# A recurrent transformer step rewritten in a fixed order by halves of heads, with part of its QKV moved into one dense pass and 42 of 64 weight chunks resident

## The chip, the cores and the metric

The kernel runs on one core of a Trainium2 chip. The metric is the device time of one execution in microseconds (us), on the slowest core, which here is the only one. Before the change the median of three runs was 2933.01 us (2913.09 to 2933.23). "The change" and "after" mean the kernel with the change; "before" the one without.

## The reference, cut to what matters

The program computes two independent outputs and puts them side by side. Part A is a long convolution by FFT; the change does not touch it, and it ends at about 279 us. Part B, the rest of the time, is this recurrence (cut):

```python
S, Dm, H, Dh, M, seg = 2048, 1024, 32, 128, 8, 32
mem = mem0                                   # 8 memory tokens
for s in range(64):                          # 64 segments of 32 tokens
    h = concat([mem, x[s*32:(s+1)*32]])      # 40 tokens x 1024
    q, k, v = h @ Wq, h @ Wk, h @ Wv         # 32 heads of 128
    p = softmax(mask(q @ k.T * Dh**-0.5))    # 40 x 40 for each head
    o = (p @ v) @ Wo                         # 40 x 1024
    mem = o[:8]                              # goes into the next segment
    outs.append(o[8:])                       # 32 tokens of output
```

Each segment needs all four weights (32 MB in bf16), and the segments follow each other through `mem`. Both kernels cut the weights into 64 chunks of 128 x 2048 (512 KB), keep some in SBUF for good ("resident") and stream the others from HBM in every segment through a ring of buffers. Both kernels feed the PE array 32 tokens at a time, so each segment's last 8 tokens are extra work and are treated apart; they don't depend on `mem` before attention.

## The kernel before

38 chunks are resident, 26 are streamed in each segment, through a ring of six. The tile scheduler orders the instructions. The last 8 tokens of the four segments of a block are taken together, as a second set of 32 rows, in the block's last segment. The softmax covers all heads in one go. The outputs are stored from the POOL (GpSimd) queue.

```python
NRES, RING = 38, 6
ring = tc.tile_pool(name="b_ring", bufs=RING)

def wchunk(m, i):
    if i in res_slot[m]:
        return res_tiles[m][:, res_slot[m][i], :]
    t = ring.tile([128, CW], BF, tag="wring", name="wchunk")
    nc.sync.dma_start(dst_view(t[:], m), dram_chunk(m, i))              # L508
    return t[:]

def qkv_pass(pairs, m, extra=None):          # pairs: this segment, and at a
    ...                                      # block's end its last 8 tokens x 4
    for kc in range(8):
        for hf in range(CPK):
            w = wchunk(m, CPK * kc + hf)
            for pi, (hT_ap, dst_sb) in enumerate(pairs):
                ...
                nc.tensor.matmul(accs[pi][g][32 * c:32 * c + 32, :], lhsT=hT_ap[:, kc, :],
                                 rhs=w[:, jl * 512:(jl + 1) * 512], ...) # L536
...
for s in range(n_seg):
    ...
    qkv_pass(qpairs, 0); qkv_pass(kpairs, 1)
    ...
    softmax(SA, masks[("A", j)], PA_pad)     # 128 x 512, all heads
    softmax(SC, masks[("C", j)], PC_pad)
    ...
    wo_pass(opairs)                          # matmuls yacc, L561
    ...
    for dq in range(4):
        nc.gpsimd.dma_start(outb[SEG * s:SEG * s + 24, dq * 256:(dq + 1) * 256],
                            Y_sb[32 * dq + 8:32 * dq + 32, :])          # L721
```

## Time and profile before

| | before |
|---|---|
| median | 2933.01 us |
| first segment's result Y copied out of PSUM | at 372.4 us |
| one segment after it (Y to Y, mean of 63) | 40.24 us |
| last segment of a block of four / the others | 45.0 / 37.3 to 39.5 us |
| bytes moved, 560 to 2860 us | 345 GB/s |

These lines are from the page of before: its span, the busy time of each engine (PE is TensorE's matmuls, PEld its weight loads, DVE VectorE, ACT ScalarE, POOL GpSimd; L508 is line 508 of the kernel), the DMA engines' busy share in 40 equal slices of the span (tenths), and the chain of waits that ended last, by engine and by line.

```profile
span 2926.3 us, 80950 instructions
...
PE 2062.4 (70%) x36046; PEld 1129.8 (39%) x36052; DVE 924.1 (32%) x1936; ACT 631.6 (22%) x1191; POOL 377.6 (13%) x714
...
DMA  7886999999999999999899998999999999999996
...
PE 40%; DMA 33%; DVE 16%; ACT 5%; issue 2%; POOL 1%; SPq 0%; ACTq 0%; DVEq 0%; POOLq 0%
DMA wchunk<-in_B_Wq_dram 17%; PE yacc L561 11%; DMA wchunk<-in_B_Wk_dram 9%; PE OTp L698 4%; PE OTp L701 3%; PE qk_tp L548 3%; DVE Ppads L592 2%; DVE ssum L590 2%; DVE mx L586 2%; ACT KA_sb L541 2%; DMA wchunk<-in_B_Wv_dram 2%; DVE SA L582 1%; ACT QA_sb L541 1%; DVE SA L587 1%; DVE SC L582 1%
```

From the fifth slice on, the DMA engines stand at 8 or 9 tenths to the last but one, while PE is busy for 70%. The chain has PE on 40% of its length and DMA on 33%. Two of its three costliest entries are loads of streamed weights, 17% and 9% of the span. So the kernel goes back and forth between the stream and PE.

The table of stretches of before shows the whole recurrence, then two short stretches inside one segment. Columns: the stretch in us, its length, busy us and instructions of PE, PEld, DVE, ACT and POOL, the granted clock (PEclk, the share of TensorE's full clock that it was given), the DMA share and GB/s.

```profile
core 0: us, PE busy (x) PEld busy (x) DVE busy (x) ACT busy (x) POOL busy (x), PEclk, DMA share, GB/s
560.00:2860.00 2300.00, 1697.20 (x31501) 953.87 (x31493) 640.27 (x1371) 412.53 (x847) 258.10 (x537) 0.85 0.95 345
1213.00:1217.00 4.00, 4.00 (x92) 3.09 (x85) 0.10 (x1) 0.00 (x0) 0.00 (x0) 0.58 0.61 205
1225.00:1241.00 16.00, 10.55 (x208) 4.60 (x211) 3.47 (x6) 2.34 (x4) 0.00 (x0) 1.00 1.02 408
```

The stream reaches 408 GB/s while PE waits for it (last line), but at 1213 to 1217 us it is down to 205. Just ahead of that PE had waited for DVE's softmax (from 1200.5 to 1208.6 us in the chain of waits) and used no chunks, so the ring was full: from 1200 to 1217 us SyncE's queue waited for PE to free a buffer for 10.4 us in all. The mean of 345 lies between. What SyncE's DMA queue, which issues the loads, waited for says the same (columns: us in total, times, longest):

```profile
SPq L508 <- PE yacc L561: 512.8, 346, 8.6
SPq L508 <- DMA wchunk<-in_B_Wq_dram: 192.2, 272, 2.8
```

The load at L508 waits mostly for matmuls, which must free a buffer of the ring: 512.8 us for those of the output projection (yacc), and 578 us for those of Q, K and V, which the view lists tile by tile. The chain of waits through the same segment, as start, length and what:

```profile
1212.82 4.50 DMA wchunk<-in_B_Wo_dram
1217.32 8.85 DMA wchunk<-in_B_Wq_dram
1226.21 0.42 PE acc_17966 L536 x4
1226.65 7.29 DMA wchunk<-in_B_Wk_dram
```

A piece such as "8.85 DMA wchunk" runs from the issue of a load to PE's use of it. With six loads in the ring one of them takes 7 to 9 us (512 KB at 408 GB/s are 1.28 us): it queues behind the others, and six at 1.28 us are 7.7. Over the whole run the loads land 6.8 to 8.1 us after their issue (medians for the four weights, from before's list of DMA issues).

### The profile page before, as it was taken

Reading aid. Unit: us, or ns where it says so; the run is one execution under the profiler, and the core shown is the slowest. Engines: PE = TensorE matmul, PEld = TensorE weight load, DVE = VectorE, ACT = ScalarE, POOL = GpSimd, SP = SyncE. Lnnn points to the kernel's source line nnn. Section 1 sums busy time; section 2 is a strip of 40 time slices with the busy share of each in tenths; the row PEclk is TensorE's granted clock in tenths of the full one; section 3 lists DMA queues with packets and bytes.
Section 4 is the critical chain, followed back from the end, with each engine's and each line's share of the span. In section 5 each row is a group of like instructions: output and inputs, shape, how many; then the busy total and the mean of one; then the engine's idle time right before and its main releaser. Section 6 shows DMA issues by size and latency. Waiting matters only on the chain.

```text
span 2926.3 us, 80950 instructions
## 1 busy us (share of the span) xinstructions
PE 2062.4 (70%) x36046; PEld 1129.8 (39%) x36052; DVE 924.1 (32%) x1936; ACT 631.6 (22%) x1191; POOL 377.6 (13%) x714
## 2 busy tenths in 40 slices
PE   3665477687776767676867777776868677777775
PEld 1221134343443434343434444343434344443433
DVE  6895122232222222222322222322232222322221
ACT  6771111121111111111111111111112111111211
POOL 4142001001010101010010101010100101010101
PEclk8897678798888889888888888798888788887977
DMA  7886999999999999999899998999999999999996
GB/s 244 305 304 229 375 334 334 341 342 362 347 335 347 331 356 345 352 331 345 330 359 351 339 350 334 348 348 363 321 349 335 348 344 332 359 335 351 348 347 234
DMA packets 356981, 979.09 MB, mean 335 GB/s; under 512 B 42556, under 2 KB 47708, under 8 KB 356631
## 3 DMA queue, kind: packets, MB, share of 16 engines
q1 hardware_dynamic: 329896, 942.33, 88.2%
q0 software_dynamic: 21504, 21.04, 2.3%
q10 hardware_dynamic: 5232, 10.55, 1.1%
q8 instruction: 282, 4.62, 0.6%
q14 instruction: 67, 0.55, 0.1%
HBM read 940.19 MB, written 33.55 MB: 333 GB/s over the span
## 4 chain that ended last, share of the span: by engine, by line
PE 40%; DMA 33%; DVE 16%; ACT 5%; issue 2%; POOL 1%; SPq 0%; ACTq 0%; DVEq 0%; POOLq 0%
DMA wchunk<-in_B_Wq_dram 17%; PE yacc L561 11%; DMA wchunk<-in_B_Wk_dram 9%; PE OTp L698 4%; PE OTp L701 3%; PE qk_tp L548 3%; DVE Ppads L592 2%; DVE ssum L590 2%; DVE mx L586 2%; ACT KA_sb L541 2%; DMA wchunk<-in_B_Wv_dram 2%; DVE SA L582 1%; ACT QA_sb L541 1%; DVE SA L587 1%; DVE SC L582 1%
## 5 line engine op out<-in xcount | busy, mean ns | idle before, releaser
L536 PEld LDWEIGHTS <-hT 128*32 128x32 bf16 x12288 | 390.8, 101 | 853.2 <-issue 614.6
L698 PE MATMUL OTp<-PTs,VA_sb 32*128 32x64 bf16 x2048 | 205.7, 232 | 143.4 <-DVE PTs L687 143.4
L549 DVE COPY QT_sb<-qk_tp 128x1024 bf16<-128x1024 bf16 x80 | 55.3, 692 | 769.7 <-PE qk_tp L548 769.7
L561 PEld LDWEIGHTS <-OT_sb 128*32 128x32 bf16 x8192 | 259.9, 121 | 82.0 <-issue 10.7
L561 PE MATMUL yacc<-Wres_2789,OT_sb 128*32 128x256 bf16 x4608 | 288.4, 338 | 1.4 <-issue 1.4
L561 PE MATMUL yacc<-wchunk,OT_sb 128*32 128x256 bf16 x3584 | 263.2, 354 | 7.1 <-DMA wchunk<-in_B_Wo_dram 5.7
L698 PEld LDWEIGHTS <-VA_sb 32*128 32x128 bf16 x2048 | 181.0, 120 | 194.1 <-issue 154.4
L721 POOL DMA_DIRECT2D out_dram<-Y_sb x256 | 128.2, 508 | 858.2 <-ACT Y_sb L565 568.0
L605 POOL COPY hT<-XT_sb 128x192 bf16<-128x192 bf16 x64 | 22.2, 347 | 1416.7 <-issue 1040.3
L549 DVE COPY KT_sb<-qk_tp 128x1024 bf16<-128x1024 bf16 x80 | 55.2, 689 | 462.3 <-PE qk_tp L548 462.3
L701 PE MATMUL OTp<-PTs,VB_sb 32*128 32x64 bf16 x2048 | 196.7, 232 | 0.5
L701 PEld LDWEIGHTS <-VB_sb 32*128 32x128 bf16 x2048 | 182.8, 122 | 0.0
L536 PEld LDWEIGHTS <-hTB 128*32 128x32 bf16 x3072 | 130.9, 98 | 70.3 <-issue 6.7
L704 ACT CAST OT_sb<-OTp 128x256 bf16<-128x256 f32 x256 | 94.9, 372 | 276.9 <-PE OTp L701 276.6
L612 DVE COPY hT<-mt_tp 128x64 bf16<-128x64 bf16 x64 | 12.3, 191 | 405.4 <-PE mt_tp L611 405.4
L726 POOL DMA_DIRECT2D out_dram<-YB_sb x256 | 126.7, 501 | 65.5 <-DMA out_dram<-Y_sb 29.4
L705 DVE CAST OTB<-OTp 128x64 bf16<-128x64 f32 x256 | 57.6, 225 | 206.0 <-ACT OT_sb L704 205.7
L565 ACT CAST Y_sb<-yacc 128x256 bf16<-128x256 f32 x64 | 23.8, 372 | 366.7 <-PE yacc L561 366.7
L548 PE MATMUL qk_tp<-ident,KA_sb 128*128 128x128 bf16 x512 | 52.6, 228 | 70.6 <-ACT KA_sb L541 70.2
L588 ACT ACTIVATE SA<-SA 128x512 f32<-128x512 f32 x64 | 37.2, 582 | 285.9 <-DVE SA L587 253.6
L548 PE MATMUL qk_tp<-ident,QA_sb 128*128 128x128 bf16 x512 | 62.3, 259 | 50.9 <-ACT QA_sb L541 50.9
L548 PEld LDWEIGHTS <-QA_sb 128*128 128x128 bf16 x512 | 35.6, 112 | 132.1 <-ACT QA_sb L541 120.4
(1731 smaller groups left out, 3917.7 us busy)
## 6 DMA issues: line engine op xcount, KB each, us to landing
wchunk<-in_B_Wv_dram SPq DMA_DIRECT2D x448, 512.0 KB, 6.8
wchunk<-in_B_Wo_dram SPq DMA_DIRECT2D x448, 512.0 KB, 7.5
wchunk<-in_B_Wq_dram SPq DMA_DIRECT2D x384, 512.0 KB, 7.0
wchunk<-in_B_Wk_dram SPq DMA_DIRECT2D x384, 512.0 KB, 8.1
SK_61<-s_sb SPq DMA_DIRECT2D x16, 512.0 KB, 4.7
SU_60<-s_sb SPq DMA_DIRECT2D x16, 512.0 KB, 3.5
Kg<-SK_61 ACTq DMA_DIRECT2D x32, 256.0 KB, 5.1
Ug<-SU_60 SPq DMA_DIRECT2D x32, 256.0 KB, 5.7
```

The lines of the kernel that those rows point to most:

```text
L536: nc.tensor.matmul(accs[pi][g][32 * c:32 * c + 32, :], lhsT=hT_ap[:, kc, :], rhs=w[:, jl * 512:(jl + 1) * 512], start=(kc == 0), stop=(kc ...
L541: nc.scalar.copy(dst_sb[:, g * 512:(g + 1) * 512], accs[pi][g][:])
L548: nc.tensor.transpose(tp[:, idx * 128:(idx + 1) * 128], src_sb[:, idx * 128:(idx + 1) * 128], ident[:])
L549: nc.vector.tensor_copy(dst[:, :, :, col0:col0 + 32], tp[:].rearrange("p (i c r) -> p i c r", i=8, c=4))
L561: nc.tensor.matmul(accs[pi][32 * dq:32 * dq + 32, 0:256], lhsT=OTsrc[:, c, idx, :], rhs=w[:, hh * 1024 + dq * 256:hh * 1024 + (dq + 1) * 256],
L582: nc.vector.scalar_tensor_tensor(out=S3, in0=S3, scalar=scale, in1=mask[:].unsqueeze(1).to_broadcast([128, 8, 64]), op0=ALU.mult, op1=ALU.add)
L586: nc.vector.tensor_reduce(out=mx[:], in_=S3, op=ALU.max, axis=AX.X)
L698: nc.tensor.matmul(OTp[:, idx, :], lhsT=VA_sb[32 * c:32 * c + 32, col:col + 128], rhs=PTA[32 * c:32 * c + 32, idx, :], start=True, stop=False,
L701: nc.tensor.matmul(OTp[:, idx, :], lhsT=VB_sb[32 * c:32 * c + 32, col:col + 128], rhs=PTB[32 * c:32 * c + 32, idx, :], start=False, stop=True,
L704: nc.scalar.copy(OT_sb[:, c, :, :], OTp[:, :, 0:32])
L721: nc.gpsimd.dma_start(outb[SEG * s:SEG * s + 24, dq * 256:(dq + 1) * 256], Y_sb[32 * dq + 8:32 * dq + 32, :])
L726: nc.gpsimd.dma_start(outb[SEG * ss + 24:SEG * ss + 32, dq * 256:(dq + 1) * 256], YB_sb[32 * dq + 8 * jj:32 * dq + 8 * jj + 8, :])
```

## The change

The intent is to take work and bytes out of a segment and pay for it once, ahead of the recurrence:

- K, Q and V of the last 8 tokens of all 64 segments are computed in one dense pass of 768 matmuls of 128 x 128 by 512 columns ahead of the recurrence. The results go to DRAM, and each segment reads its part back (256 KB in seven small reads).
- 42 chunks are resident instead of 38, so 22 are streamed instead of 26. The ring falls from six to four. 24 of the residents ("late") take the memory that the dense pass had used, and are loaded when it has ended.
- The recurrence is in a fixed order instead of the scheduler's, by halves of 16 heads, so that one half's softmax runs beside the other half's projections. The softmax pass is 128 x 320.
- Y is stored in one transfer, from ScalarE's (ACT) queue instead of POOL's.

Part B is rewritten in whole; this is the core of the diff, with cuts marked by "..." and a few comments with line numbers added:

```diff
+NSTREAM = 22
+NEARLY = 18
+RING = 4
...
-    NRES = cfg.get("nres", 38)
-    RING = cfg.get("ring", 6)
...
+        for m in (0, 1):                       # dense pass: K and Q, then V alike
+            for g in range(2):
+                ws = group(m, g)
+                stage = st.tile([128, n_seg, 16, 8], BF, tag="stage", name="stage")
+                for hl in range(16):
+                    ps = ps0.tile([128, 512], F32, tag="ps0", name="kb_ps")
+                    for kc in range(8):
+                        nc.tensor.matmul(ps[:], lhsT=ws[kc][:, hl * 128:(hl + 1) * 128],
+                                         rhs=XBT[:, kc].rearrange("p s t -> p (s t)"), ...)
...
+                nc.sync.dma_start(dst[g], stage[:].rearrange("p s h t -> p s (h t)"))
...
+    def fetch():
+        n = len(loaded)
+        if n < len(uses):
+            t = ring.tile([128, 2048], BF, tag="wring", name="wring")
+            nc.sync.dma_start(dst_view(t[:], uses[n]), dram_chunk(uses[n]))      # L554
+            loaded.append(t)
...
+    def load_x(s):
+        hT = two.tile([128, 8, SEG], BF, tag="hT", name="hT")
+        nc.sync.dma_start(hT[:].rearrange("p k t -> p (k t)"), XTD[:, s]...)     # L575
+        KBs = two.tile([128, 2, 128], BF, tag="KBs", name="KBs")
+        nc.sync.dma_start(KBs[:], KBD[:, :, s, :].rearrange("g p n -> p g n"))
+        QBs = two.tile([128, 288], BF, tag="QBs", name="QBs")
+        nc.sync.dma_start(QBs[:, 0:256]..., QBD[:, :, s, :].rearrange("g p n -> p g n"))
...
+    with tc.manual_schedule():
+        for _ in range(RING):
+            fetch()
...
+            for c in range(4):
+                nc.sync.dma_start(VBs[32 * c:32 * c + 8, :], VBD[s, c])          # L607
...
+            k0 = evac_qk(proj(0, 0))
+            q0 = evac_qk(proj(1, 0))
+            if s + 1 < n_seg:
+                load_x(s + 1)
+            transposes(k0, KTs[0][:, :, :, 0:32])
...
+            S0 = scores(0, QT0)
+            PT0 = softmax(S0)
+            transposes(k1, KTs[1][:, :, :, 0:32])
+            a_v0 = proj(2, 0)
...
+            attend(0, PT0, V, OTp)
+            evac_o(0, OTp, OT)
+            PT1 = softmax(S1)
...
+            out_proj(0)
+            attend(1, PT1, V, OTp)
+            evac_o(1, OTp, OT)
+            out_proj(1)
...
+            nc.scalar.dma_start(bass.AP(outb.tensor, outb.offset + SEG * s * 2048, [[256, 4], [2048, 32], [1, 256]]), Y[:])
...
-        for dq in range(4):
-            nc.gpsimd.dma_start(outb[SEG * s:SEG * s + 24, dq * 256:(dq + 1) * 256], Y_sb[32 * dq + 8:32 * dq + 32, :])
```

## The prediction

> **What bounds the kernel now.** From about 371 us to the end the program is 63 of 64 recurrent segments, 40.5 us each. The page shows PE 70% and DVE 32% busy over the span; the table of stretches gives DMA share 0.94 to 0.95 and 342 to 348 GB/s from 400 to 2800 us. The chain of waits agrees: 17% waiting for Wq chunks, 9% for Wk. A segment streams 26 chunks of 512 KB (13.6 MB, the list of issues: 1664 loads). Inside one segment, 1225 to 1241 us ran at 403 to 412 GB/s; at 1213 to 1217 us the share was 0.61: the ring of six was full after PE had waited for the softmax (8.1 us of DVE, 1200.5 to 1208.6). So: the weight stream, plus gaps when the ring is full. [...]
>
> **What the change does per segment.**
> - Removes 4 of 26 chunks: 4 x 1.28 us at 408 GB/s is 5.1 us, 5.9 us at the stage's mean of 344.
> - Removes the extra QKV matmuls of block ends (about 10 us of PE every fourth segment), partly hidden now.
> - Adds about 800 small packets a segment (X, K, Q, V of the last 8 tokens from DRAM). The software queue's took about 50 ns each; over 16 engines about 2.4 us, against 1.3 us for today's output and X.
> - Splits softmax. A 128x512 DVE pass takes 0.69 us; a 128x320 one I estimate at 0.49, so one half's chain is about 4.1 us (estimate: five passes, exp 0.42, reciprocal 0.18, two transposes 0.82). But in the fixed order the second K transpose's copy stands behind softmax 0 on DVE, and softmax 1 behind the first half's attention. So PE stands about 2.5 us before the second Q transposes and about 2.5 us before the second attention, and the ring, now four, fills.
> - PE alone: 48 groups of four 512-wide matmuls at 0.215 us, 32 of 256 at 0.108, transposes, scores, attention: about 20 us, 27 to 29 with those stands.
>
> DMA work is 22 x 1.28 to 1.42 + 2.4 = 31 to 34 us; with the bursts not overlapping perfectly (before: about 15% over its own minimum) I take 35.0 us a segment, saving 5.5 x 64 = 350 us.
>
> **What it costs ahead.** Today the recurrence gets going at about 335 us, after 38 chunks. After: 18 early chunks and X (14 MB, about 40 us from 275), then 768 dense 512-wide matmuls at 0.216 us, 166 us, all critical; then 24 late chunks, whose space is the pass's own, 12.6 MB, about 31 us with PE idle. The recurrence starts near 525 us: +190 us.
>
> **Sum.** 525 + 64 x 35.0 = 2765 us. Range 2655 to 2880. Faster by over 2%: 0.86; within 2%: 0.12; slower: 0.02.
>
> **What would show it.** A dense pass of 165 to 180 us with PE at 9 tenths, PE idle for about 30 us, recurrence from 510 to 540 us. Segments of 34 to 36 us with DMA share 0.88 to 0.95; PE's longest waits still for ring chunks; two on DVE, 2 to 3 us each, per segment.
>
> **What would make it wrong.** Small packets costing more; a ring of four too shallow, segments of 37 us and over (then little gained); or the attention on four row groups overlapping fully and the stream holding 408 GB/s (33 us, 2640).

The estimates can be followed from the trace of before. A line through DVE's cast of 128 x 64 (0.225 us, L705) and its pass of 128 x 512 (0.69) gives 0.49 at 320 columns; one through ACT's cast of 128 x 256 (0.37, L704) and the exp of 128 x 512 (0.58, L588) gives 0.42. The reciprocal took 0.18 and a transpose of 128 x 256 0.40 to 0.43. Groups of four 512-column matmuls began 0.217 us apart (median, L536), and part A's 512-column matmuls 0.215 to 0.216 where nothing held them up; 0.108 is half of that. The 21,504 packets of the software queue took 2.3% of 16 engines' span, so 50 ns each. The record gives no source for the 1.42 us of a chunk; it comes to 369 GB/s, between the 345 and the 408 of the table of stretches.

## The result, and the profile after

The change made the kernel slower: 3158.7 us median of four runs (3156.76 to 3169.99) against 2933.12 of before in the same rounds, a ratio of 1.0778 with a 95% interval of 1.0738 to 1.0819. A ratio here and below is the mean time of one kernel's fast runs over that of the other's of the same rounds, so it is not quite the ratio of the medians quoted.

| | before | predicted | after |
|---|---|---|---|
| time | 2933 us | 2765 us | 3158.7 us |
| first Y | 372.4 us | 525 + 35 = 560 us | 599.7 us |
| one segment (mean of the 63 that follow) | 40.24 us | 35.0 us | 40.43 us |
| GB/s over the recurrence | 345 | none given | 295 |

The miss of 394 us is made up as follows: first Y 40 us late, 63 x (40.43 - 35.0) = 342 us in the segments, and 12 us between the last Y and the time of the run. Against before, the start costs 227 us, and the segments, which were to earn it back, are no shorter although they load four chunks fewer.

The page of after, the same lines as of before:

```profile
span 3154.7 us, 75437 instructions
...
PE 2005.4 (64%) x33470; PEld 972.8 (31%) x33492; DVE 846.0 (27%) x1940; ACT 577.5 (18%) x1015; POOL 126.8 (4%) x294
...
DMA  7869446888988888988898989888989888888887
...
DMA 52%; PE 23%; DVE 11%; ACT 4%; issue 3%; POOL 0%; SPq 0%; ACTq 0%; POOLq 0%; DVEq 0%
DMA wring<-in_B_Wq_dram 15%; DMA wring<-in_B_Wk_dram 11%; DMA out_dram<-Y 11%; PE acc L620 7%; DMA wring<-in_B_Wo_dram 6%; PE yacc L701 6%; PE kb_ps L513 3%; DMA wring<-in_B_Wv_dram 3%; ACT OT L687 2%; DVE PT L668 2%; PE vb_ps L526 1%; PE ybacc L701 1%; DVE S L658 1%; DVE ssum L662 1%; DVE P_pad L664 1%
```

PE is busy for a smaller share, DMA too, and yet the chain is now 52% DMA. A new entry stands in the chain, as long as the loads of Wk: the store of the result, "out_dram<-Y", 11%. The table of stretches (columns as above), for the recurrence, for the dense pass and for the gap after it:

```profile
core 0: us, PE busy (x) PEld busy (x) DVE busy (x) ACT busy (x) POOL busy (x), PEclk, DMA share, GB/s
600.00:3146.00 2546.00, 1648.40 (x31390) 814.82 (x31394) 581.55 (x1464) 365.18 (x693) 40.15 (x185) 0.82 0.87 295
330.00:517.00 187.00, 171.89 (x776) 77.70 (x790) 34.72 (x51) 29.48 (x52) 0.00 (x0) 0.97 0.42 148
517.00:558.00 41.00, 0.44 (x3) 0.13 (x2) 1.10 (x3) 0.00 (x0) 0.13 (x1) 0.55 0.94 347
```

The dense pass and the gap have the shape that was predicted: 187 us at a busy PE, then 41 us in which PE stands and the late chunks come in at 347 GB/s. The recurrence is where the account fails: a DMA share of 0.87 moves only 295 GB/s. What SyncE's queue waited for in the recurrence:

```profile
SPq L554 <- PE acc L620: 470.9, 628, 3.2
SPq L554 <- DMA wring<-in_B_Wq_dram: 273.5, 268, 4.0
...
SPq L554 <- DMA out_dram<-Y: 105.7, 48, 3.6
...
SPq L607 <- DMA out_dram<-Y: 60.3, 15, 4.8
...
SPq L554 <- DMA out_dram<-YB: 36.9, 29, 1.8
```

As before, most of it is for PE to free a buffer, or for loads ahead. New are the last three lines: the queue that issues the weights stands 203 us in all (105.7 + 60.3 + 36.9) until a store of Y or YB has landed, with which it shares no data. What PE waited for:

```profile
PE acc L620 <- DMA wring<-in_B_Wq_dram: 346.8, 289, 5.8
PE acc L620 <- DMA wring<-in_B_Wk_dram: 131.2, 129, 3.4
...
PE qk_tp L634 <- DVE KT L635: 82.7, 62, 1.9
...
PE OTp L677 <- DVE PT L668: 29.0, 30, 2.1
```

The first two lines and those for Wo (64.7) and Wv (38.5) add up to 581 us of waiting for ring chunks, 9.2 us a segment. The two stands on DVE that the prediction expected of the fixed order (the last two lines) are a fifth of that. The chain through one segment's end and the next one's start:

```profile
1250.18 0.38 ACT Y L746
1250.59 5.09 DMA out_dram<-Y
...
1255.74 6.36 DMA wring<-in_B_Wk_dram
...
1262.14 0.42 PE acc L620 x4
1262.58 5.63 DMA wring<-in_B_Wq_dram
...
1268.26 0.43 PE acc L620 x2
```

Y is ready at 1250.6 us; 5.1 us go by until its store has landed; only then is a Wk load issued that takes 6.4 us to be used, and a Wq load after that takes 5.6 us. Where before has its 7 to 9 us for a load once or twice a segment, after runs from one such round trip to the next.

The store is issued from ACT's queue and the loads from SP's, yet the trace shows SP's queue standing for it: 48 loads for a store of Y (2.2 us each), 29 for one of YB (1.3 us each), and 15 reads of VBs for one of Y (4.0 us each). In the chain above SP stands 1.5 us for the store, to 1255.7 us, and in that time the trace has no other issue of SP's. Why a load waits for a store of another queue is left aside here, as the views quoted do not show it; what happens when the stores leave ACT's queue was put to an experiment.

### The profile page after: what moved, and what is told of

Read it like the earlier page. It is cut to its first block, busy times and chain, and to the rows that moved or that the text cites. A ratio compares the mean times of both kernels' runs of the same rounds, so it can differ in the third digit from the quotient of the medians.

```text
span 3154.7 us, 75437 instructions
## 1 busy us (share of the span) xinstructions
PE 2005.4 (64%) x33470; PEld 972.8 (31%) x33492; DVE 846.0 (27%) x1940; ACT 577.5 (18%) x1015; POOL 126.8 (4%) x294
## 4 chain that ended last, share of the span: by engine, by line
DMA 52%; PE 23%; DVE 11%; ACT 4%; issue 3%; POOL 0%; SPq 0%; ACTq 0%; POOLq 0%; DVEq 0%
DMA wring<-in_B_Wq_dram 15%; DMA wring<-in_B_Wk_dram 11%; DMA out_dram<-Y 11%; PE acc L620 7%; DMA wring<-in_B_Wo_dram 6%; PE yacc L701 6%; PE kb_ps L513 3%; DMA wring<-in_B_Wv_dram 3%; ACT OT L687 2%; DVE PT L668 2%; PE vb_ps L526 1%; PE ybacc L701 1%; DVE S L658 1%; DVE ssum L662 1%; DVE P_pad L664 1%
## 5 line engine op out<-in xcount | busy, mean ns | idle before, releaser
L620 PE MATMUL acc<-wring,hT 128*32 128x512 bf16 x4096 | 497.4, 471 | 526.3 <-DMA wring<-in_B_Wq_dram 348.8
L620 PE MATMUL acc<-Wearly,hT 128*32 128x512 bf16 x4608 | 476.2, 484 | 22.2 <-DVE hT L587 21.9
L628 ACT CAST qk_sb<-acc 128x512 bf16<-128x512 f32 x256 | 149.9, 585 | 1258.1 <-PE acc L620 1126.0
L701 PE MATMUL yacc<-Wlate,OT 128*32 128x256 bf16 x5120 | 291.0, 326 | 102.3 <-ACT OT L687 101.3
L620 PE MATMUL acc<-Wlate,hT 128*32 128x512 bf16 x3584 | 347.6, 452 | 0.0
L701 PEld LDWEIGHTS <-OT 128*32 128x32 bf16 x8192 | 250.7, 113 | 238.9 <-ACT OT L687 115.1
L701 PE MATMUL yacc<-wring,OT 128*32 128x256 bf16 x3072 | 197.8, 324 | 66.6 <-DMA wring<-in_B_Wo_dram 65.4
L634 PE MATMUL qk_tp<-ident,qk_sb 128*128 128x128 bf16 x1024 | 123.6, 257 | 85.6 <-DVE KT L635 84.9
L668 DVE STREAM_TRANSPOSE PT<-P_pad 128x256 bf16<-128x256 bf16 x256 | 98.7, 424 | 4.4
L513 PE MATMUL kb_ps<-XBT,Wearly 128*128 128x512 bf16 x282 | 84.1, 379 | 1.4 <-ACT XBT L482 1.2
```

The source lines that it names most:

```text
L513: nc.tensor.matmul(ps[:], lhsT=ws[kc][:, hl * 128:(hl + 1) * 128], rhs=XBT[:, kc].rearrange("p s t -> p (s t)"), start=(kc == 0), stop=(kc ...
L620: nc.tensor.matmul(acc[32 * c:32 * c + 32, :], lhsT=hT[:, kc, :], rhs=w[:, c * 512:(c + 1) * 512], start=(kc == 0), stop=(kc == 7), tile_p ...
L628: nc.scalar.copy(sb[:], acc[:])
L634: nc.tensor.transpose(tp[:, i * 128:(i + 1) * 128], sb[:, i * 128:(i + 1) * 128], ident[:])
L668: nc.vector.transpose(out=PT[:, kb].rearrange("p i (a q) -> p (i a) q", a=2), in_=P_pad[:].rearrange("p i a k -> p (i a) k")[:, :, 32 * kb ...
L701: nc.tensor.matmul(acc[32 * dq:32 * dq + 32, 0:256], lhsT=src[:, c, idx, :], rhs=w[:, hh * 1024 + dq * 256:hh * 1024 + (dq + 1) * 256], st ...
```

## The experiments

Four theories were put to the test.

- Queues: the stores and small reads hold up the stream, as its loads stand in SP's queue until they have landed. The recorded texts call this Theory A.
- Depth: a ring of four chunks is too small to keep the DMA engines at their rate, and too small a store for the times when PE uses none.
- Small packets: the reads and stores of the last 8 tokens cost more than estimated.
- DVE order: the stands that the fixed order puts before PE are what a segment waits for.

Medians, and ratios to before in the same rounds with their 95% intervals:

| run | queues of stores / small reads | streamed, ring | median us | ratio | us per segment |
|---|---|---|---|---|---|
| after | ACT / SP | 22, 4 | 3158.7 | 1.0778 [1.0738, 1.0819] | 40.4 |
| e1_store_pool | POOL / SP | 22, 4 | 3064.98 | 1.0451 [1.0423, 1.0480] | 39.0 |
| e2_no_store * | none / SP | 22, 4 | 3058.88 | 1.0440 [1.0395, 1.0484] | 38.9 |
| e5_store_read_pool | POOL / POOL | 22, 4 | 3054.85 | 1.0418 [1.0380, 1.0456] | 38.8 |
| e7_no_small_reads * | POOL / none | 22, 4 | 3009.06 | 1.0265 [1.0186, 1.0344] | 37.8 |
| e3_no_stream * | ACT / SP | 0 | 2398.21 | 0.8185 [0.8155, 0.8215] | 28.6 |
| e4_ring6 | ACT / SP | 24, 6 | 3104.75 | 1.0605 [1.0571, 1.0639] | 39.6 |
| e10_ring8_same_bytes * | ACT / SP | 22, 8 | 2853.59 | 0.9734 [0.9689, 0.9779] | 35.8 |
| e11_ring8_same_bytes_pool * | POOL / POOL | 22, 8 | 2652.42 | 0.9048 [0.9001, 0.9095] | 32.6 |
| e8_all_pool_ring6 | POOL / POOL | 24, 6 | 2908.27 | 0.9911 [0.9887, 0.9935] | 36.5 |
| e9_ring8_26 | POOL / POOL | 26, 8 | 2919.86 | 0.9954 [0.9931, 0.9977] | 36.8 |
| e12_half_chunks | POOL / POOL | 22, 8 halves | 3020.22 | 1.0303 [1.0270, 1.0335] | 38.1 |
| e13_half_24_ring12 | POOL / POOL | 24, 12 halves | 2932.8 | 0.9997 [0.9971, 1.0023] | 36.9 |
| e14_dve_order | POOL / POOL | 22, 4 | 3075.38 | 1.0509 [1.0462, 1.0556] | 39.0 |
| e18_trim_22_ring4 | POOL / POOL | 22, 4 | 3049.77 | 1.0421 [1.0379, 1.0463] | 38.5 |
| e17_trim_22_ring5 | POOL / POOL | 22, 5 | 2848.48 | 0.9753 [0.9693, 0.9814] | 35.5 |
| e20_trim_22_ring5_order | POOL / POOL | 22, 5 | 2820.98 | 0.9632 [0.9584, 0.9680] | 34.9 |
| e15_trim_23_ring6 | POOL / POOL | 23, 6 | 2799.79 | 0.9568 [0.9522, 0.9614] | 34.7 |
| e16_trim_23_ring6_order | POOL / POOL | 23, 6 | 2741.36 | 0.9361 [0.9314, 0.9408] | 33.9 |

Runs marked * give a wrong result; all others are correct. Those were taken in one round (two runs), the others in three (four runs).

### First set: which part of a segment is the stream, and are the stores in its way?

**e1_store_pool** moves the stores of Y and YB back to POOL's queue.

```diff
-            nc.scalar.dma_start(bass.AP(outb.tensor, ...), Y[:])
+            nc.gpsimd.dma_start(bass.AP(outb.tensor, ...), Y[:])
...
-                    nc.scalar.dma_start(        # YB, the same
+                    nc.gpsimd.dma_start(
```

> One edit: the stores of Y and YB are issued from the POOL queue, as the kernel before did, not from ACT; same bytes, same rows. Theory A ([...]a ring load has to wait until a small, slow store has landed; the trace shows SP waiting for out_dram<-Y and out_dram<-YB for about 216 us in the recurrence): those waits vanish from the SP queue and the time falls by 120 to 220 us, to about 2940 to 3040. Rival B (a ring of four is too shallow): within 40 us of 3159. Rival C (the fixed order makes PE stand): within 40 us of 3159.

Measured: 3064.98 us, 94 us below after, and outside the range expected, on the side of a smaller effect. Among SP's waits from 600 to 2640 us none for a store is left. The queues theory is right, but at a ring of four it is not the main cause.

**e2_no_store** leaves out all stores but the last segment's (wrong).

```diff
+            if s == n_seg - 1: nc.scalar.dma_start(bass.AP(outb.tensor, ...), Y[:])
...
-                for dq in range(4):
+                for dq in range(4 if s == n_seg - 1 else 0):
```

> Wrong result on purpose: Y and YB are stored in the last segment alone. Theory A: at least the gain of e1_store_pool, 150 to 250 us below 3159, and it bounds what the stores cost in all, their own packets included. [...] Rivals B and C: within 60 us of 3159.

Measured: 3058.88 us, the same as e1 within the intervals, and 100 us below after where 150 to 250 were expected. So it was not the stores' bytes or packets that cost 94 us, but their place in the queues: on POOL they cost nothing that can be seen.

**e3_no_stream** takes resident chunks for the streamed ones (wrong).

```diff
-        return loaded[used[0]]
+        return res[resident[order.index(ch) % len(resident)]]
...
     def done(ch):
-        if ch in streamed:
-            loaded[used[0]] = None
-            used[0] += 1
-            fetch()
+        pass
```

> Wrong result on purpose: no ring loads at all, each streamed chunk is replaced by a resident one; order of work, small reads and stores stay. It measures the recurrence without the stream. Theory A and B: 27 to 30 us a segment (total 2280 to 2500). Rival C (the order on PE, DVE and ACT bounds it): 36 us or more a segment.

Measured: 2398.21 us, and 28.6 us a segment. That is what PE, ACT and DVE need when no weights are waited for, and within the 27 to 29 of the prediction. What PE waits for most in e3, over its recurrence:

```profile
PE qk_tp L628 <- DVE KT L629: 158.4, 64, 3.7
...
PE OTp L671 <- DVE PT L662: 78.0, 48, 2.1
```

Divided by 64 segments these are 2.5 and 1.2 us: the stands on DVE that the prediction put at about 2.5 us each are real, but in after they are mostly hidden behind the stream.

**e4_ring6** has a ring of six as before has, and pays for it with two chunks more to stream.

```diff
-NSTREAM = 22
+NSTREAM = 24
-RING = 4
+RING = 6
```

> Ring of 6 instead of 4, paid for by 24 streamed chunks instead of 22 (40 resident), so the same memory. Two more chunks are 2.6 to 2.9 us of stream a segment. Rival B: the deeper ring more than pays, time falls by 60 us or more. Theory A: no gain, the same to 180 us slower[...].

Measured: 3104.75 us, 54 us below after (short of the 60 that were expected of depth), in spite of 1 MB more in every segment. Depth is worth more than the bytes, but with after's queues the gain is small.

### Second set: depth and queues apart

**e5_store_read_pool** moves the small reads to POOL's queue as well, on top of e1, so that SP issues weights alone.

```diff
 # on e1
-        nc.sync.dma_start(hT[:]..., XTD[:, s]...)
+        nc.gpsimd.dma_start(hT[:]..., XTD[:, s]...)
 # the same for KBs, QBs and the four of VBs
```

> Stores and the small reads (X, K, Q, V of the last 8 tokens, 7 transfers a segment) all issued from the POOL queue, so that the SP queue carries ring loads alone[...]; ring of 4, 22 streamed. Theory A in its wide form[...]: 30 to 100 us below e1_store_pool (3065), SP's waits on transfers near zero. Rival B (four slots are the limit, whatever the queue): within 30 us of e1_store_pool.

The wide form of the theory is that the small reads hold up the loads as the stores do.

Measured: 3054.85 us. The 10 us against e1 are inside the intervals, so at a ring of four nothing is shown for the reads' queue.

**e7_no_small_reads** leaves the small reads out from the third segment on (those of V from the second), on top of e1 (wrong).

```diff
 # on e1
+        if s > 1:
+            pend[s] = keep[s % 2]
+            return
...
-            for c in range(4):
+            for c in range(4 if s == 0 else 0):
```

> Wrong result on purpose: stores on POOL as in e1_store_pool, and the small reads are made for the first two segments alone, later segments use those tiles. It bounds the small reads' cost[...]. If their packets cost what I estimated (2 us a segment): about 130 us below e1_store_pool, so 2935;[...] if nothing: 3065.

Measured: 3009.06 us, 56 us below e1, or 0.9 us a segment. The prediction's 2.4 us a segment for all small packets was no underestimate, so the theory of small packets falls. The 56 us hold the reads' packets and their place in the queue together; with packets as estimated, 2935 us was expected.

**e10_ring8_same_bytes** has a ring of eight with 22 streamed chunks. The memory is found by letting the last four resident chunks share one place (wrong; four loads fall away ahead of the recurrence, and the first Y comes 9 us sooner than in after). Queues are after's.

```diff
-RING = 4
+RING = 8
-    late = resident[NEARLY:]
+    late = resident[NEARLY:-4]
+    for ch in resident[-4:]:
+        res[ch] = wlate_t[:, len(late) - 1, :]
```

> Wrong result on purpose: 22 streamed chunks and the changed kernel's queues, but a ring of 8, its memory gained by letting four resident Wo chunks share the place of another (4 loads of 512 KB less ahead, about 5 us). Rival B (depth): 120 to 250 us below 3159. Theory A alone[...]: less than 80 us below.

**e11_ring8_same_bytes_pool** is e10 with e5's queues.

```diff
 # on e10: load_x, VBs and the stores as in e5
-        nc.sync.dma_start(hT[:]..., XTD[:, s]...)
+        nc.gpsimd.dma_start(hT[:]..., XTD[:, s]...)
...
-            nc.scalar.dma_start(bass.AP(outb.tensor, ...), Y[:])
+            nc.gpsimd.dma_start(bass.AP(outb.tensor, ...), Y[:])
```

> Wrong result on purpose: e10's ring of 8 with e5's queues. If A and B are both at work: clearly below e5 and e10, 34 to 36 us a segment, 2740 to 2860 in all, where my prediction stood. If only B: the same as e10. If only A: the same as e5.

Measured: 2853.59 and 2652.42 us. Depth alone, at the same bytes, is worth 305 us with after's queues and 402 us with the queues of e5. Of this, 9 and 12 us lie ahead of the first Y. Both gains are above what was expected (120 to 250 us for e10, and 2740 to 2860 us for e11). The queues are worth 104 us at a ring of four (after to e5) and 201 us at a ring of eight (e10 to e11). One line of what SP's queue waits for in e10 shows the two at odds (L609 is the read of VBs, L607 in after; the stretch is 600 to 2640 us):

```profile
SPq L609 <- DMA out_dram<-Y: 293.4, 57, 6.8
```

The read of VBs waits 57 times, 5.1 us each, for a store of Y to land, and the loads behind it stand. In e11 no such line is left. The table of stretches for e5, the recurrence and 8 us in which PE waited for the stream for about half of the time:

```profile
600.00:2640.00 2040.00, 1365.06 (x26158) 677.02 (x26151) 486.08 (x1222) 305.41 (x579) 317.08 (x635) 0.83 0.90 309
1241.00:1249.00 8.00, 4.07 (x84) 1.95 (x83) 3.76 (x9) 1.59 (x3) 0.00 (x0) 1.00 0.97 352
```

And for e11, the recurrence and 15 us in which PE waited for a smaller part:

```profile
600.00:2640.00 2040.00, 1456.01 (x31188) 784.35 (x31184) 581.65 (x1462) 363.97 (x690) 368.27 (x738) 0.87 1.00 366
1257.00:1272.00 15.00, 11.65 (x216) 5.31 (x212) 4.83 (x12) 2.67 (x5) 0.00 (x0) 0.67 1.03 393
```

In these short stretches the stream runs at 352 GB/s with a ring of four and at 393 with eight, near the 408 of before. Over the recurrence it is 309 against 366 GB/s. The DMA records of the kept traces, summed over all of PE's waits for chunks from 600 to 2640 us, give 319 GB/s in e5 and 376 in e11; over the rest of the time it is 306 and 365. So a ring of four is slow even while PE asks for chunks, and the deeper ring raises the rate in both kinds of time. e11's segment of 32.6 us, with a DMA share of 1.00, is within the prediction's 31 to 34 us for the DMA work.

**e8_all_pool_ring6** is e5 with a ring of six and 24 streamed, which fits in memory and is correct.

```diff
 # on e5
-NSTREAM = 22
+NSTREAM = 24
-RING = 4
+RING = 6
```

> Correct result. Stores and small reads on POOL, 24 streamed chunks, ring of 6. If depth and the queue together set the rate: stream near e11's 366 GB/s, 12.9 MB a segment, 35.2 to 36.5 us, 2820 to 2910 in all, below before's 2931. If depth alone: near e4_ring6 less a little, 3050.

**e9_ring8_26** goes on along the same line: a ring of eight with 26 streamed.

```diff
 # on e5
-NSTREAM = 22
+NSTREAM = 26
-RING = 4
+RING = 8
```

> Correct result. As e8 but 26 streamed chunks and a ring of 8: the kernel before's number of streamed chunks. If the stream saturates (366 GB/s): 13.9 MB is 38 us a segment, 2980 to 3020; slower than e8, since depth past saturation only costs bytes. If depth still pays at 6 to 8: below e8.

Measured: 2908.27 us (as expected) and 2919.86 us (below the expectation, as the stream came to 381 GB/s over 600 to 2640 us). The table of stretches for e8:

```profile
600.00:2640.00 2040.00, 1404.20 (x27900) 730.71 (x27893) 517.58 (x1302) 325.23 (x616) 336.16 (x672) 0.84 0.98 357
```

From 309 GB/s at four to 357 at six: the kernel is 147 us faster than e5 with 1 MB more to load in each segment. At eight the further rate only pays for the further megabyte. Against e4, which differs in the queues alone, e8 is 196 us faster: as at eight, the queues matter more where the ring is deeper.

### Third set: number of loads or number of bytes? And the order on DVE

**e12_half_chunks** loads halves of 256 KB into a ring of eight halves: as many bytes under way as in e5, in twice as many loads.

```diff
 # on e5
-RING = 4
+RING = 8
-    uses = [ch for s in range(n_seg) for ch in order if ch in streamed]
+    uses = [(ch, hf) for s in range(n_seg) for ch in order if ch in streamed for hf in range(2)]
...
-            t = ring.tile([128, 2048], BF, tag="wring", name="wring")
+            t = ring.tile([128, 1024], BF, tag="wring", name="wring")
...
 # weight(ch, hf) gives a half; done(ch) after each half
```

> Correct result. Queues of e5, 22 streamed chunks, but each streamed in two halves of 256 KB with a ring of 8 halves: the same 2 MB of ring. If what matters is the number of loads under way and how early a slot comes free: 34 to 36 us a segment, 2740 to 2870. If what matters is the bytes that the ring holds: as e5_store_read_pool, 3055 within 40 us.

**e13_half_24_ring12** is the same at 24 streamed and 12 halves, the bytes of e8's ring.

```diff
 # on e12
-NSTREAM = 22
+NSTREAM = 24
-RING = 8
+RING = 12
```

> Correct result. e12's halves with 24 streamed chunks and a ring of 12 halves (3 MB). Stream saturated: 35.2 us a segment, 2815 to 2850. If bytes in the ring matter and not their number: as e8.

Measured: 3020.22 us, 35 us below e5, and 2932.8 us, 24 us above e8 and a miss of its range. The tables of stretches for e12 and for e13:

```profile
600.00:2640.00 2040.00, 1448.51 (x26504) 681.96 (x26508) 490.64 (x1234) 309.54 (x586) 322.63 (x646) 0.89 0.94 313
```

```profile
600.00:2640.00 2040.00, 1488.56 (x27470) 714.87 (x27463) 508.47 (x1279) 319.99 (x606) 327.83 (x657) 0.91 1.01 351
```

313 GB/s, hardly above e5's 309: twice the loads in the same 2 MB bring almost nothing. So there the bytes that the ring holds count, and not how many loads they are cut into. e13's ring holds 12 halves (3 MB), the bytes of e8's, and comes to 351 GB/s against 357. What SP's queue waited for, in e12 and in e13:

```profile
SPq L556 <- PE acc L623: 674.3, 1112, 3.7
...
SPq L556 <- DMA wring<-in_B_Wq_dram: 56.4, 101, 1.6
```

```profile
SPq L556 <- PE acc L623: 185.7, 448, 1.5
SPq L556 <- DMA wring<-in_B_Wv_dram: 181.4, 562, 1.7
```

With the loads of the other weights, SP waited 100 us for its own loads in e12 and 653 us in e13. The author's reading was that not all 12 halves can be under way at once; that was not shown, as the waits don't tell how many are (in e5, with four chunks in the ring, SP waited 634 us for its own loads). Against e12 the four halves more brought 313 GB/s to 351, with two chunks more to stream, and SP stands less for the matmuls of Q, K and V to release one (186 us against 674).

**e14_dve_order** is e5 with the second K half's transposes ahead of the first softmax on DVE, and the second softmax ahead of the first half's copies of O.

```diff
 # on e5
-            PT0 = softmax(S0)
             transposes(k1, KTs[1][:, :, :, 0:32])
+            PT0 = softmax(S0)
...
-            evac_o(0, OTp, OT)
             PT1 = softmax(S1)
+            evac_o(0, OTp, OT)
```

> Correct result. e5's queues, ring of 4, 22 streamed; the only edit is order: the second K transposes and their copy go ahead of softmax 0, and softmax 1 goes ahead of the first half's output copies, so that PE no longer stands behind DVE there (1.3 us and 0.5 us a segment in the trace of the changed kernel). If the ring's bytes set the rate (bytes under way over a round trip): within 40 us of e5_store_read_pool (3055). If the ring is short because it must bridge PE's stands, or if the order bounds (rival C): 60 to 130 us below e5.

Measured: 3075.38 us, 20 us above e5, with intervals that just do not meet. What PE waited for, from 600 to 2640 us, in e5:

```profile
PE acc L620 <- DMA wring<-in_B_Wq_dram: 272.9, 245, 3.2
...
PE qk_tp L634 <- DVE KT L635: 55.3, 49, 1.9
```

And in e14:

```profile
PE acc L620 <- DMA wring<-in_B_Wq_dram: 272.0, 236, 3.1
...
PE S L642 <- DVE QT L635: 72.1, 52, 2.2
```

The wait for KT has gone, a wait for QT has come in its place, and the wait for Wq is as before. So the edit moved the stands on DVE more than it removed them: PE's waits for DVE's KT, QT, PT and OTB are 103 us in e5 and 91 in e14. What speaks against the theory of the DVE order at a ring of four is their size: 103 us in e5 against 433 us of waits for chunks.

### Fourth set: one slot of depth by itself, and the best version that fits

**e15_trim_23_ring6** frees memory: hT, KBs, QBs and Y get one buffer instead of two, Y0 shares Y's, and `load_x` of the next segment moves behind V. That gives a ring of six with 23 streamed.

```diff
 # on e5
-NSTREAM = 22
+NSTREAM = 23
-RING = 4
+RING = 6
-        hT = two.tile([128, 8, SEG], BF, tag="hT", name="hT")
+        hT = one.tile([128, 8, SEG], BF, tag="hT", name="hT")
 # the same for KBs, QBs and Y; Y0 takes Y's tag
...
 # load_x(s + 1) moved from behind q0 to behind V
```

> Correct result. As e17 with 23 streamed and a ring of 6. Between e8 (24 streamed, ring 6: 2908) and one chunk less at 1.3 us a segment: 2810 to 2850, over 2% faster than before.

**e16_trim_23_ring6_order** is e15 with e14's order.

```diff
 # on e15
-            PT0 = softmax(S0)
             transposes(k1, KTs[1][:, :, :, 0:32])
+            PT0 = softmax(S0)
...
-            evac_o(0, OTp, OT)
             PT1 = softmax(S1)
+            evac_o(0, OTp, OT)
```

> Correct result. e15 with e14's order. Order matters only where the stream doesn't: 0 to 50 us below e15.

**e17_trim_22_ring5** has 22 streamed and a ring of five, **e18_trim_22_ring4** is its control with a ring of four, and **e20_trim_22_ring5_order** is e17 with e14's order.

```diff
 # e17, on e15
-NSTREAM = 23
+NSTREAM = 22
-RING = 6
+RING = 5
 # e18, on e17
-RING = 5
+RING = 4
```

> Correct result. e5's queues, 22 streamed, ring of 5: one slot more, its memory from single instead of double buffers for the small inputs and outputs (loaded after V instead of after Q). Bytes under way: a quarter more of them, 120 to 200 us below e5, 2860 to 2935. If depth only helped at 8 (bridging long stands): 2990 or more.

> Correct result. Control for e17: its single buffers and its later time of the small reads, but a ring of 4 as in e5. If the slot made e17's gain: within 40 us of e5 (3055). If the later reads made it: near e17 (2848).

```diff
 # e20, on e17: as e16 on e15
-            PT0 = softmax(S0)
             transposes(k1, KTs[1][:, :, :, 0:32])
+            PT0 = softmax(S0)
...
-            evac_o(0, OTp, OT)
             PT1 = softmax(S1)
+            evac_o(0, OTp, OT)
```

> Correct result. e17 (22 streamed, ring of 5) with e14's order. Order cost 20 us at a ring of 4 and gained 58 at 6 with 23 streamed; here I expect 0 to 50 us below e17, so 2800 to 2850, above e16 (2741).

Measured: e18 3049.77 us, so the freed memory and the moved loads do nothing by themselves (e5: 3054.85). e17 2848.48 us, below its range: one slot more is worth 201 us, with correct results and nothing else changed. The tables of stretches for e18 and for e17:

```profile
600.00:2640.00 2040.00, 1341.95 (x26350) 668.44 (x26354) 489.88 (x1232) 307.40 (x583) 318.95 (x635) 0.85 0.91 311
```

```profile
600.00:2640.00 2040.00, 1379.73 (x28495) 721.37 (x28494) 531.49 (x1336) 333.23 (x632) 343.54 (x683) 0.88 0.95 337
```

311 against 337 GB/s at the same bytes in each segment. e15 came to 2799.79 us, a little below its range. The order that cost 20 us at a ring of four gained 27 us at five (e20) and 58 us at six (e16; 50 at most was expected). There the stream hid less of the stands on DVE, and the edit removed more: from 142 us in e15 to 95 in e16. The table of stretches for e16:

```profile
600.00:2640.00 2040.00, 1397.98 (x30004) 720.56 (x30003) 550.35 (x1400) 345.67 (x663) 362.27 (x720) 0.91 1.00 369
```

At 2741.36 us e16 is the best correct version: 6.4% faster than before and 13% faster than after (2741.36 over 3158.7). Its DMA share is 1.00 at 369 GB/s, so the stream is again what bounds it most.

## Why the prediction was wrong

The change was predicted at 2765 us and measured at 3158.7.

**The step that failed** is the last one of the sum for a segment: "DMA work is 22 x 1.28 to 1.42 + 2.4 = 31 to 34 us; with the bursts not overlapping perfectly (before: about 15% over its own minimum) I take 35.0 us a segment". It takes a duration for a chunk that the trace of before showed with six chunks in the ring, and uses it for a ring of four. The segment measured 40.43 us. 342 of the 394 us of the miss are here.

What the runs showed in its place:

- The size of the ring set the rate. With the queues cleared, four, five and six chunks in the ring gave 309, 337 and 357 GB/s, and eight 366 to 381, over the same stretch. At 22 streamed chunks the step from four to five alone is worth 201 us (e18 to e17). As an estimate, a slot's turn at four is 4 x 524,288 B over 309 GB/s = 6.8 us, of which the four transfers at 408 GB/s would need 5.1. By this estimate the remaining 1.7 us, release, issue and landing with the times when the ring is full, are not covered by other loads, and a deeper ring covers more of them. With 12 halves in place of eight, SP stood 186 us instead of 674 for the matmuls of Q, K and V to free a slot (e13, e12).
- The new stores and reads stood in the loads' way. The prediction counted them as packets (2.4 us a segment) and did not ask in which queue they stand. Their place cost 104 us at a ring of four and 201 us at eight. e2 shows for the stores that it is the place and not the packets.
- The risk was named ("a ring of four too shallow, segments of 37 us and over (then little gained)") but got 2% of the chances for a slower kernel, though the trace of before showed what is needed: a round trip of 7 to 9 us with six loads in it.

Point by point, the rest:

- "The recurrence starts near 525 us: +190 us": first Y at 599.7 against 560 foreseen (525 + 35), +227 against before. The dense pass took 183 us (334 to 517) for 166, of which PE waited 12.5 us for its own Wv chunks; PE stood for 41 us ahead of the recurrence instead of 31; the first segment took 41.7 us (558 to 599.7) instead of 35. These are 34 of the 40 us. They were read from the trace and not put to an experiment. They are terms of the right kind and too small a size.
- "PE alone: about 20 us, 27 to 29 with those stands": right, 28.6 in e3. The two stands on DVE of "about 2.5 us" measured 2.5 and 1.2 us there; in after they were 1.3 (82.7 us over 63) and 0.5, hidden by the stream.
- The DVE pass of 128 x 320, estimated at 0.49 us, took 0.50 to 0.51 in the chain, and exp 0.42 to 0.43. Right.
- "DMA work 31 to 34 us": right as a floor, 32.6 in e11, but after did not come near it.
- "Segments of 34 to 36 us with DMA share 0.88 to 0.95": the share was 0.87, close to the range, with a segment of 40 us. The share of busy DMA engines was only a loose measure of the rate: 0.87 went with 295 GB/s, 0.95 with 345 in before.
- "PE's longest waits still for ring chunks": right, 9.2 us a segment.
- The attention on four row groups, which the prediction left as a chance for better, did overlap. Before, which takes one row group after another, starts the matmuls of its attention 0.05 us apart (median); after, with the row groups in turn, starts the 32 of a half within 0.2 to 0.5 us, 6 to 16 ns apart, though each takes 0.18 us by the profile. In the dense pass of after, where weight loads and matmuls all use 128 rows, the loads (98 ns each) begin within 3 ns of the start of a matmul (739 of 768), and the matmuls start 216 ns apart (median, granted clock 0.97), as predicted. The overlap in the attention gained nothing here, as it is not what a segment waits for.

What stays open: how much of the ring's effect comes from bytes under way and how much from slots in reserve (e13 was not meant to test it, streams 24 chunks against e12's 22, and how many of its halves were under way at once was not shown); which part of a round trip (release by PE, issue, queueing, landing) is the one that a ring of four doesn't cover; whether stores on ACT's queue would be harmless if no load of SP's waited for them; and how the 201 us of the queues at a ring of eight divide between stores and reads.

## What to carry to other kernels

Memory taken from a stream's ring to keep more data resident can cost more than the bytes it saves: before trading, look in the trace at how long a load takes from issue to use, and how long the loads wait for a free buffer. Keep the queue that feeds the critical stream free of every transfer that can wait for something else, and look in the trace whether it stands for transfers of another queue, as SP's here for the stores of ACT's (203 us in after, none left in e1). Reordering compute may pay only after the stream is out of the way: here the same edit cost 20 us with a ring of four and gained 58 with six.
